# The first four attention chunks loaded on two queues, with three warming products instead of seven

## The chip, the cores and the metric

The kernel runs on one core of one Trainium2 chip. A core has TensorE (PE), VectorE (DVE), ScalarE (ACT), GpSimd (POOL) and SyncE (SP); each works through its own list of instructions in order. SyncE and ScalarE also issue DMAs, each on a hardware queue of its own. The metric is the device time of one execution in microseconds.

## The reference

Inputs q, k, v have the shape (4, 8, 576, 64): batch, heads, tokens, head size. The first stage is attention with a decay for each head and no softmax; two feed-forward layers follow, on 2304 tokens with 512 columns.

```python
scores = (1 / sqrt(64)) * q @ k^T
ret = scores * where(rel >= 0, gamma_h ** rel, 0)      # gamma_h = 1 - 2 ** (-5 - h)
x = (ret @ v).transpose(0, 2, 1, 3).reshape(2304, 512)
h = x @ moe_w_in                                       # 512 -> 2048
y = softplus(h) @ moe_w_out                            # 2048 -> 512
r = relu(y @ moe2_w_in)                                # 512 -> 2048
out = (r * r) @ moe2_w_out                             # 2048 -> 512
```

The weights come as float64 and are passed as pairs of 32-bit words; the kernel turns them into 32-bit parts itself. The launch also passes q and k stacked by dims (qk_t), k and v stacked by tokens (kv), and one small array of constants.

## The kernel before

Attention runs in chunks of 128 tokens, two pieces of 64 (s = 0, 1), over 8 heads. It is done in its recurrent form: each chunk has scores inside the chunk, a masked product with v, and a state that is carried to the next chunk. The first feed-forward layer takes its tokens in three tiles of 512, 384 and 384, and the remaining tokens go through a block later. The first tile needs chunks 0 to 3, so these are done ahead of everything else, in an order written out by hand (the block under `tc.manual_schedule()`, lines 1431 to 1510). Later chunks are loaded by `load_chunk` into a ring and worked in between the products of the feed-forward layer.

For an early chunk c:

- `early_qk(c)` (L1267) loads 512 KB of q and k in two DMAs: the lower four heads go to partitions 0 to 63, the upper four to partitions 64 to 127. `early_kv(c)` (L1276) loads 512 KB, k in column block 0 and v in block 1, in one DMA over 128 partitions. All of these are on SyncE's queue.
- `early_scores(c)` (L1281) makes 32 products on PE from both halves of qk. Even chunks write the tile pb, odd ones two other banks.
- `early_mask(c)` (L1304) multiplies the scores by the causal mask on VectorE; `early_v(c)` (L1297) scales v.
- `early_states(c)` (L1317) adds k^T v to the state on PE; ScalarE copies it (`kept`, L1329).
- `early_carried(c)` and `early_o(c)` make the output po on PE, from the kept state and from the masked scores. The tile po has one buffer, which `spread_rows` uses first, under the name rows.
- `early_x(c)` (L1352) multiplies po by a table in cst on VectorE (L1361), and ScalarE rounds the result (xh, L1366); `early_low(c)` makes the rest (xl, L1372).

The tables in cst are made on the chip. Two rows of constants are loaded (rows_in, L1442), `spread_rows` (L1407) spreads them over the partitions with eight products, ScalarE copies the result out (L1420, L1421), and `make_xw` on VectorE (L1248) and `scalar_xw` on ScalarE (L1426) make the tables of the later pieces.

`keep_warm(n)` (L1228) makes n products of a zero tile into a bank that nobody reads. There are six ahead of the scores of chunk 0 and one behind `spread_rows`.

Behind the chunks' loads SyncE issues the first three loads of w_in (L142, by `pump_load(3)`) and the loads of chunk 4 (L430). `begin_words` and what it starts turn a loaded piece of weights into words: two instructions on ScalarE (L172, L173), two on VectorE (L178, L181, tile ct), then a rounding on ScalarE (L226) and a difference on VectorE (L227). The first products of the feed-forward layer are in `early_g1` (L1391) and `g1` (L594).

Each DMA of the two hardware queues counts its landing on one of eight semaphores, which it takes in turn.

Of the kernel before, what the change touches and what calls it, by code (L numbers as in the profile page):

```python
# [18 lines left out]
CN = 64  # L19
# [30 lines left out]
C_ONE, C_UP, C_VW, C_MASK, C_XW = 0, 1, 2, 74, 138  # L50
# [4 lines left out]
def kernel(  # L55
# [26 lines left out]
    nc = tc.nc  # L82
# [261 lines left out]
    def pump_load(upto):  # L344
        while n_load[0] < min(upto, len(loads)):
            load_w(*loads[n_load[0]])
            n_load[0] += 1
# [72 lines left out]
    LO, HI = slice(0, P // 2), slice(P // 2, P)  # L420
# [5 lines left out]
    def load_chunk(c, queue=nc.sync):  # L426
        if c < NPR:
            new_chunk(c)
            for i, src in ((0, qk_t), (2, kv)):
                queue.dma_start(  # L430
                    out=chunk[c][:, i:i + 2],
                    in_=src[2 * c:2 * c + 2].rearrange("s p i h c -> (s p) i h c"),
                )
# [794 lines left out]
    def keep_warm(count, n=512):  # L1228

        for _ in range(count):  # L1230
            nc.tensor.matmul(
                cold[:, :n], lhsT=warm[:, :P], rhs=warm[:, :n], start=True, stop=True
            )
# [11 lines left out]
    def make_xw(m, n):  # L1245


        nc.vector.scalar_tensor_tensor(  # L1248
            out=later[:, m - 1:m - 1 + n],
            in0=cst[:, x_first].rearrange("p (a b) -> p a b", a=KD).unsqueeze(1)  # L1250
            .to_broadcast([P, n, KD, CN]),
            scalar=1.0,
            in1=times[:, m - 1:m - 1 + n].unsqueeze(3).to_broadcast([P, n, KD, CN]),
            op0=ALU.mult, op1=ALU.mult,
        )
# [4 lines left out]
    qks, kvs, mixed, kept_s, pbs, pos, xs_of = {}, {}, {}, {}, {}, {}, {}  # L1260
    causal = first_pool.tile([P, P], F32, tag="causal", name="causal", bufs=1)

    def early_tiles(c):
        qks[c] = first_pool.tile([P, 2, 2, HH, CN], F32, tag=f"qk{c}", name="qk", bufs=1)
        kvs[c] = first_pool.tile([P, 2, H, CN], F32, tag=f"kv{c}", name="kv", bufs=1)

    def early_qk(c):  # L1267
        for g, half in enumerate((LO, HI)):
            nc.sync.dma_start(
                out=qks[c][half].rearrange("p i s h c -> p i s (h c)"),  # L1270
                in_=qk_t[2 * c:2 * c + 2].rearrange("s p i h c -> p i s (h c)")[
                    ..., g * HH * CN:(g + 1) * HH * CN
                ],
            )

    def early_kv(c):  # L1276
        nc.sync.dma_start(
            out=kvs[c], in_=kv[2 * c:2 * c + 2].rearrange("s p i h c -> (s p) i h c")
        )

    def early_scores(c):  # L1281
        if c % 2:
            pb = pbs[c] = [ps_h.tile([P, 512], F32, tag=f"h{g}", name="pb") for g in range(2)]
        else:
            pb = ps_head.tile([P, 2, 512], F32, tag="pb", name="pb", bufs=1)
            pbs[c] = [pb]
            pb = [pb[:, g] for g in range(2)]
        for hh in range(HH):
            for s, to in enumerate((LO, HI)):
                for g, rows in enumerate((LO, HI)):  # L1290
                    nc.tensor.matmul(
                        pb[g][to, hh * P:(hh + 1) * P],
                        lhsT=qks[c][rows, 1, s, hh, :], rhs=qks[c][rows, 0, :, hh, :],
                        start=True, stop=True, skip_group_check=True,
                    )

    def early_v(c):  # L1297
        t = kvs[c][:, 1]
        w = vw[:, 2 * c * H:(2 * c + 1) * H]
        nc.vector.tensor_tensor(  # L1300
            out=t, in0=t, in1=w.unsqueeze(2).to_broadcast([P, H, D]), op=ALU.mult
        )

    def early_mask(c):  # L1304
        mixed[c] = first_pool.tile([P, H, P], F32, tag="mixed", name="mixed")
        for g, pb in enumerate(pbs[c]):
            n = H // len(pbs[c])
            if len(pbs[c]) == 1:
                pb = pb.rearrange("p g (h n) -> p (g h) n", n=P)
            else:  # L1310
                pb = pb.rearrange("p (h n) -> p h n", n=P)
            nc.vector.tensor_tensor(
                out=mixed[c][:, g * n:(g + 1) * n], in0=pb,
                in1=causal.unsqueeze(1).to_broadcast([P, n, P]), op=ALU.mult,
            )
# [29 lines left out]
    def early_o(c):  # L1345
        for hh in range(H):
            nc.tensor.matmul(
                early_po(c, hh), lhsT=kvs[c][:, 1, hh, :], rhs=mixed[c][:, hh, :],
                start=c == 0 and hh % HH < 2, stop=True, skip_group_check=True,
            )  # L1350
# [56 lines left out]
    def spread_rows():  # L1407
        rows = ps_head.tile([P, 2, 512], F32, tag="po", name="rows", bufs=1)
        to = [
            rows[:, 0, at:at + n * b].rearrange("p (a b) -> p a b", a=n)  # L1410
            for at, n, b in ((0, KD, CN), (256, SCN - 1, KD))
        ]
        for half in (LO, HI):
            one = slice(half.start, half.start + 1)
            for r, of in zip(to, (row[0][:, 0], row[0][:, 1:, :, 0])):
                nc.tensor.matmul(
                    r[half], lhsT=ones[one], rhs=of[one],
                    start=r is to[0], stop=True, skip_group_check=True,
                )
        nc.scalar.copy(cst[:, x_first].rearrange("p (a b) -> p a b", a=KD), to[0])  # L1420
        nc.scalar.mul(times, to[1], float(D) ** 0.5)  # L1421

    def scalar_xw(m, n):
        for m in range(m, m + n):
            for a in range(KD):
                nc.scalar.activation(  # L1426
                    out=later[:, m - 1, a], in_=cst[:, C_XW + a * CN:C_XW + (a + 1) * CN],
                    func=AF.Copy, scale=times[:, m - 1, a:a + 1],
                )

    with tc.manual_schedule():
        rows_in = xs.tile([P, SCN * KD * CN], F32, tag="xr", name="rows_in")
        for c in range(last):
            early_tiles(c)
        early_qk(0)
        for half in (LO, HI):
            nc.scalar.dma_start(out=cst[half, :C_XW], in_=consts[CN:P, :C_XW])
        early_kv(0)
        early_qk(1)
        early_kv(1)  # L1440
        for r in (0, CN):
            nc.scalar.dma_start(out=rows_in[r:r + 1], in_=consts[r:r + 1, C_XW:])  # L1442
        nc.scalar.preload_act_table_set("softplus")
        for c in range(2, last):
            early_qk(c)
            early_kv(c)
        pump_load(3)
        load_chunk(last)
        nc.vector.memset(causal[LO, CN:], 1.0)
        nc.vector.memset(causal[HI, :CN], 0.0)  # L1450

        for half, to, of, n in ((LO, 0, 0, SCN), (HI, 0, 1, SCN - 1), (HI, SCN - 1, 0, 1)):
            nc.vector.tensor_copy(
                vw[half, to * H:(to + n) * H], cst[half, C_VW + of * H:C_VW + (of + n) * H]
            )
        for s, half in enumerate((LO, HI)):
            nc.vector.tensor_copy(
                causal[half, s * CN:(s + 1) * CN], cst[half, C_MASK:C_MASK + CN]
            )
        keep_warm(6)  # L1460
        early_scores(0)
        row.append(rows_in.rearrange("p (m a b) -> p m a b", a=KD, b=CN))
        spread_rows()
        keep_warm(1)
        scalar_xw(4, 2)
        early_mask(0)
        early_v(0)
        make_xw(1, 1)
        early_scores(1)
        early_states(0)  # L1470
        early_mask(1)
        early_v(1)
        early_carried(0)
        early_o(0)
        early_x(0)
        early_scores(2)
        early_states(1)
        scalar_xw(6, 1)
        early_carried(1)
        early_o(1)  # L1480
        make_xw(2, 2)
        early_mask(2)
        early_v(2)
        early_x(1)
        scalar_xw(7, 2)
        early_scores(3)
        early_states(2)
        early_carried(2)
        early_o(2)
        early_low(0)  # L1490
        early_mask(3)
        early_v(3)
        begin_words()
        early_x(2)
        next(begun[0])
        early_low(1)
        early_states(3)
        early_carried(3)
        early_o(3)
        next(begun[0])  # L1500
        begun.clear()
        begin_words()
        early_g1(0)
        early_x(3)
        next_state(3, 1)
        begin_words()
        early_low(2)
        early_low(3)
        for made in begun:
            next(made)  # L1510
# [228 lines left out]
```

## Time and profile before

| what | value |
|---|---|
| runs | 817.22, 819.52, 819.86 us; median 819.52 |
| profiled execution | 820.17 us |
| its span, first to last instruction | 818.3 us |
| PE busy | 803.6 us, 98% of the span |
| DVE, ACT, POOL busy | 654.5, 402.5, 29.8 us |
| mean granted TensorE clock | 1.00 |
| DMA | 201.97 MB, mean 247 GB/s |

All times inside the span count from its first instruction. Busy times come from one profiled execution. An engine name with a q (SPq, ACTq) is that engine's sequencer, which issues DMAs; PEld is the loading of weights into PE, which overlaps with PE's products. A row of the timeline merges neighbouring instructions of one line and counts them (x2).

### The profile page before, as it was taken

How to read it: one execution, taken by the hardware profiler on the slowest of the kernel's cores; microseconds unless marked ns; L12 is line 12 of the kernel's file. 1: busy time of each engine (PE TensorE's matmuls, PEld its weight loads, DVE VectorE, ACT ScalarE, POOL GpSimd, SP SyncE). 2: the span in 40 equal slices, each digit the busy share in tenths (PEclk: the TensorE clock that was granted, in tenths of full speed). 3: DMA queues.
4: the chain of work that ended last, by engine and by line, in shares of the span. 5: the costliest groups of instructions: out<-in, count | busy, mean ns of one | idle time of the engine just before them, and what ended most of it. 6: DMA issues, size and time to landing. Idle time of an engine off the chain costs nothing.

```text
span 818.3 us, 16414 instructions
## 1 busy us (share of the span) xinstructions
PE 803.6 (98%) x5909; PEld 710.6 (87%) x5909; DVE 654.5 (80%) x1255; ACT 402.5 (49%) x781; POOL 29.8 (4%) x74
## 2 busy tenths in 40 slices
PE   8899999999899999999999999999999999999998
PEld 5678888988899888788888999988999988999887
DVE  4889886668547799977779698988798997897876
ACT  3888874555345456666666311554211554111553
POOL 0000111111110100000000000000000000000000
PEclk9999999999999999999999999999999999999999
DMA  9766776899557234459898987898988788987885
GB/s 238 267 195 210 258 248 229 291 306 322 204 195 238 94 116 146 140 171 348 280 318 298 314 278 252 268 291 281 296 253 249 250 274 264 298 248 249 254 271 172
DMA packets 124467, 201.97 MB, mean 247 GB/s; under 512 B 10850, under 2 KB 68834, under 8 KB 123618
## 3 DMA queue, kind: packets, MB, share of 16 engines
q1 hardware_dynamic: 118208, 179.87, 69.0%
q10 hardware_dynamic: 3620, 12.67, 4.7%
q0 software_dynamic: 2560, 8.39, 2.6%
q8 instruction: 47, 0.77, 0.4%
q14 instruction: 32, 0.26, 0.1%
HBM read 153.71 MB, written 47.19 MB: 245 GB/s over the span
## 4 chain that ended last, share of the span: by engine, by line
PE 74%; DMA 12%; DVE 8%; ACT 4%; issue 2%; SPq 0%; ACTq 0%; DVEq 0%
PE py L733 9%; PE py L806 9%; PE acc L628 8%; PE ph L594 8%; PE px L733 6%; PE pz L806 6%; PE px L806 6%; PE pz L733 6%; PE acc L1185 5%; PE py L1051 3%; DMA o2d<-ct 2%; DMA ring<-in_kv_dram 2%; DMA wo_raw<-in_moe_w_out_dram 2%; PE px L1051 2%; PE pz L1051 2%
## 5 line engine op out<-in xcount | busy, mean ns | idle before, releaser
L628 PE MATMUL acc<-gh,wo 128*128 128x384 f32 (+1 forms) x384 | 115.9, 362 | 0.6 <-ACT gh L612 0.6
L733 PE MATMUL py<-t,sring 128*128 128x384 f32 x432 | 88.3, 338 | 0.0
L594 PE MATMUL ph<-xh,wi 128*128 128x384 f32 (+1 forms) x376 | 80.4, 354 | 3.4 <-DVE ring L469 1.4
L628 PEld LDWEIGHTS acc<-gh,wo 128*128 128x128 f32 x384 | 70.8, 188 | 8.2 <-ACT gh L612 1.3
L733 PEld LDWEIGHTS py<-t,sring 128*128 128x128 f32 x432 | 74.8, 188 | 2.7 <-DVE uring L937 0.7
L594 PEld LDWEIGHTS ph<-xh,wi 128*128 128x128 f32 x376 | 67.0, 188 | 10.5 <-issue 2.0
L628 PE MATMUL acc<-gl,wo 128*128 128x384 f32 (+1 forms) x192 | 68.4, 356 | 1.3 <-DVE gl L613 1.3
L754 DVE TENSOR_TENSOR gl<-g,gh 128x384 fp32r<-128x384 f32 (+1 forms) x100 | 57.4, 575 | 11.2 <-ACT gh L786 8.0
L754 DVE TENSOR_TENSOR gring<-g,gring 128x384 fp32r<-128x384 f32 (+1 forms) x100 | 57.1, 575 | 11.5 <-ACT gring L786 9.0
L786 ACT CAST gh<-g 128x384 fp32r<-128x384 f32 x84 | 43.1, 515 | 46.6 <-PE px L806 16.7
L786 ACT CAST gring<-g 128x384 fp32r<-128x384 f32 x84 | 43.1, 514 | 40.3 <-PE py L806 16.4
L733 PE MATMUL pz<-t,sring 128*128 128x384 f32 x288 | 58.8, 334 | 0.0
L733 PE MATMUL px<-t,sring 128*128 128x384 f32 x288 | 58.3, 335 | 0.0
L933 ACT COPY uring<-px 128x384 f32<-128x384 f32 x24 | 11.5, 481 | 87.8 <-PE px L733 87.8
L754 DVE TENSOR_TENSOR g<-g 128x384 f32<-128x384 f32 x96 | 52.4, 554 | 1.4
L733 PEld LDWEIGHTS px<-t,sring 128*128 128x128 f32 x288 | 50.5, 188 | 0.6 <-ACT uring L933 0.5
L733 PEld LDWEIGHTS pz<-t,sring 128*128 128x128 f32 x288 | 50.8, 188 | 0.0
L469 DVE TENSOR_TENSOR ring<-pb,cst 64x256 f32<-64x256 f32 x56 | 23.6, 421 | 28.0 <-PE pb L459 16.4
L1185 PE MATMUL acc<-gring,wo 128*128 128x512 f32 x192 | 44.8, 389 | 0.0
L245 ACT CAST ct<-ct 128x512 fp32r<-128x512 f32 (+1 forms) x53 | 30.2, 570 | 28.1 <-DVE ct L181 15.6
L594 PE MATMUL ph<-xl,wi 128*128 128x384 f32 (+1 forms) x188 | 43.5, 352 | 0.0
L605 ACT ACTIVATE e<-ph 128x384 f32<-128x384 f32 (+1 forms) x48 | 25.2, 525 | 35.9 <-issue 19.5
(165 smaller groups left out, 1778.0 us busy)
## 6 DMA issues: line engine op xcount, KB each, us to landing
sring<-s2d SPq DMA_DIRECT2D x168, 256.0 KB, 3.3
sring<-o2d SPq DMA_DIRECT2D x168, 256.0 KB, 3.5
wi_raw<-in_moe_w_in_dram SPq DMA_DIRECT2D x32, 512.0 KB, 6.2
wo_raw<-in_moe_w_out_dram SPq DMA_DIRECT2D x32, 512.0 KB, 4.1
o2d<-ct SPq DMA_DIRECT2D x48, 256.0 KB, 3.2
s2d<-ct SPq DMA_DIRECT2D x33, 256.0 KB, 3.8
ring<-in_qk_t_dram ACTq DMA_DIRECT2D x12, 512.0 KB, 5.6
ring<-in_kv_dram ACTq DMA_DIRECT2D x12, 512.0 KB, 7.7
```

The costliest lines, as they stand in the source:

```text
L245: nc.scalar.copy(h, src)
L469: nc.vector.tensor_tensor(out=chunk[c][rows, 1, i * HH:(i + 1) * HH], in0=pb[of], in1=mask[of], op=ALU.mult)
L594: nc.tensor.matmul(ph[:, :n], lhsT=a, rhs=x, start=(j == 0), stop=(j == len(todo) - 1))
L605: nc.scalar.activation(out=g, in_=hps.pop(key)[:, :n], func=AF.Softplus)
L628: nc.tensor.matmul(acc[j][:, :n], lhsT=a, rhs=x, start=(begin and m == 0), stop=(end and m == 2))
L733: nc.tensor.matmul(ps, lhsT=a, rhs=x, start=(first and m == 0), stop=(m == len(todo) - 1), skip_group_check=True,)
L754: nc.vector.tensor_tensor(out=out, in0=a, in1=b, op=ALU.subtract)
L786: nc.scalar.copy(h, src)
L806: nc.tensor.matmul(blocks[m][:, :cols], lhsT=a[:, c], rhs=x, start=(first and p == n == 0), stop=(p == NP - 1 and n == len(todo) - 1), ski ...
L933: nc.scalar.copy(s1, px)
L1051: nc.tensor.matmul(ps, lhsT=a, rhs=x, start=(first and m == 0), stop=(m == len(todo) - 1), skip_group_check=True,)
L1185: nc.tensor.matmul(accs[half][j], lhsT=a[:, c], rhs=x, start=(begin and m == 0), stop=(end and m == 2),)
```

## The change

The lower heads of qk and all of k stay on SyncE's queue; the upper heads and v go to ScalarE's. kv becomes two DMAs of 256 KB. The two loads of rows_in are issued ahead of the kv of chunk 0 instead of behind the kv of chunk 1. `keep_warm(6)` becomes `keep_warm(3)`, and the `keep_warm(1)` behind `spread_rows` is gone. On ScalarE the order is then: upper qk of chunk 0, two loads of constants, two of rows, v of chunk 0, upper qk and v of chunk 1, the loading of the activation table (L1443), and upper qk and v of chunks 2 and 3; what ScalarE computes comes behind these.

```diff
     def early_qk(c):
-        for g, half in enumerate((LO, HI)):
-            nc.sync.dma_start(
+        for g, (half, queue) in enumerate(((LO, nc.sync), (HI, nc.scalar))):
+            queue.dma_start(
                 out=qks[c][half].rearrange("p i s h c -> p i s (h c)"),
                 in_=qk_t[2 * c:2 * c + 2].rearrange("s p i h c -> p i s (h c)")[
                     ..., g * HH * CN:(g + 1) * HH * CN
...
     def early_kv(c):
-        nc.sync.dma_start(
-            out=kvs[c], in_=kv[2 * c:2 * c + 2].rearrange("s p i h c -> (s p) i h c")
-        )
+        for i, queue in enumerate((nc.sync, nc.scalar)):
+            queue.dma_start(
+                out=kvs[c][:, i],
+                in_=kv[2 * c:2 * c + 2, :, i].rearrange("s p h c -> (s p) h c"),
+            )
...
         early_qk(0)
         for half in (LO, HI):
             nc.scalar.dma_start(out=cst[half, :C_XW], in_=consts[CN:P, :C_XW])
+        for r in (0, CN):
+            nc.scalar.dma_start(out=rows_in[r:r + 1], in_=consts[r:r + 1, C_XW:])
         early_kv(0)
         early_qk(1)
         early_kv(1)
-        for r in (0, CN):
-            nc.scalar.dma_start(out=rows_in[r:r + 1], in_=consts[r:r + 1, C_XW:])
         nc.scalar.preload_act_table_set("softplus")
...
-        keep_warm(6)
+        keep_warm(3)
         early_scores(0)
         row.append(rows_in.rearrange("p (m a b) -> p m a b", a=KD, b=CN))
         spread_rows()
-        keep_warm(1)
         scalar_xw(4, 2)
```

## Rows read from the trace of the kernel before

**Rows 1.** The page, engines: busy us (share of the span) and instructions.

```profile
PE 803.6 (98%) x5909; PEld 710.6 (87%) x5909; DVE 654.5 (80%) x1255; ACT 402.5 (49%) x781; POOL 29.8 (4%) x74
```

**Rows 2.** Windows: stretch, length, busy per engine (instructions), granted clock, DMA share, GB/s.

```profile
core 0: us, PE busy (x) PEld busy (x) DVE busy (x) ACT busy (x) POOL busy (x), PEclk, DMA share, GB/s
...
9.73:17.86 8.13, 7.73 (x168) 5.53 (x160) 6.42 (x9) 4.06 (x15) 0.00 (x0) 1.00 1.08 259
20.65:24.60 3.95, 3.62 (x89) 2.97 (x88) 3.16 (x5) 3.59 (x11) 0.00 (x0) 1.00 1.09 406
12.65:19.60 6.95, 6.47 (x143) 4.94 (x138) 5.68 (x9) 3.37 (x12) 0.00 (x0) 1.00 1.05 272
19.63:23.69 4.06, 3.71 (x94) 2.98 (x86) 2.81 (x5) 4.06 (x12) 0.00 (x0) 1.00 1.08 394
24.73:40.69 15.96, 13.70 (x79) 10.55 (x77) 13.72 (x21) 12.60 (x23) 0.00 (x0) 1.00 0.69 228
40.69:100.00 59.31, 59.31 (x489) 47.95 (x490) 53.30 (x88) 50.02 (x89) 1.57 (x4) 1.00 0.68 215
```

**Rows 3.** Chain of waits, first 80 us: start, us, what the end waited for.

```profile
2.29 7.44 DMA kv<-in_kv_dram
9.74 9.15 DMA qk<-in_qk_t_dram
...
40.69 2.83 PE ph L594 x11
```

**Rows 4.** Timeline, DMA issues of SyncE and ScalarE: start, us, engine, line.

```profile
0.74 1.20 ACTq L1437 DMA_DIRECT2D cst<-in_consts_dram  x2
0.74 1.50 SPq L1269 DMA_DIRECT2D qk<-in_qk_t_dram  x2
...
4.78 0.34 SPq L1277 DMA_DIRECT2D kv<-in_kv_dram  x1
```

**Rows 5.** DMA view, issues at 0.74, 1.52 and 4.78: KB, us to landing.

```profile
qk<-in_qk_t_dram SPq DMA_DIRECT2D x1, 256.0 KB, 4.0
...
qk<-in_qk_t_dram SPq DMA_DIRECT2D x1, 256.0 KB, 4.4
...
kv<-in_kv_dram SPq DMA_DIRECT2D x1, 512.0 KB, 9.0
```

**Rows 6.** Waits of SyncE's queue, 0 to 20 us: total, times, longest us.

```profile
SPq L1269 <- DMA kv<-in_kv_dram: 2.3, 1, 2.3
```

**Rows 7.** Timeline, PE and its weight loads, 1 to 10 us.

```profile
1.46 7.93 PE L1231 MATMUL cold<-warm 128*128 128x512 f32 x12 [1.46 <-DVE warm L1225]
...
5.88 0.34 PEld L1231 LDWEIGHTS cold<-warm 128*128 128x128 f32 x1 [0.52 <-issue]
...
6.65 0.19 PEld L1231 LDWEIGHTS cold<-warm 128*128 128x128 f32 x1 [0.43 <-issue]
...
9.31 1.10 PE L1291 MATMUL pb<-qk 64*64 64x128 f32 x32
```

**Rows 8.** Timeline, ScalarE and VectorE, 3 to 25 us.

```profile
3.04 1.28 ACT L1443 ACT_TABLE_LOAD   x1 [3.04 <-issue]
...
11.17 0.37 ACT L1420 COPY cst<-rows 128x256 f32<-128x256 f32 x1 [6.84 <-PE rows L1416]
11.44 0.20 ACT L1421 ACTIVATE times<-rows 128x32 f32<-128x32 f32 x1
...
12.23 0.42 DVE L1248 SCALAR_TENSOR_TENSOR cst<-cst,times 128x256 f32<-128x256 f32 x1
...
24.73 0.69 DVE L181 SCALAR_TENSOR_TENSOR ct<-wi_raw 128x512 uint32<-128x512 uint32 x1
```

## The prediction

> **What bounds the kernel now.** I read the page first. PE is busy 98% of the span [rows 1], so on the whole a microsecond is gained only where PE waits, or where work ahead of its stream ends sooner. The windows then cut the span: from 40.69 us on PE has no gap (59.31 busy of 59.31), while between 24.73 and 40.69 it is busy 13.70 of 15.96 and VectorE 13.72, ScalarE 12.60 [rows 2]. The chain of waits says what leads up to 40.69: a transfer of kv until 9.73, one of qk until 18.89, then work on VectorE and ScalarE until PE's first unbroken product at 40.69 [rows 3]. So the change is worth what it moves 40.69, and that shift should last: behind it the transfers are issued by what the engines finish and would move along.
>
> Two things hold the head of the kernel. One is the transfer rate. The loads of chunks 0 to 3 move 259 GB/s from 9.73 to 17.86, with the DMA share above 1; the weights behind them move 406 GB/s from 20.65 to 24.60 [rows 2]. kv of chunk 0 lands at 9.73 and kv of chunk 1 at 4.78 + 9.0 = 13.78, so a chunk of 1 MB takes 4.05 us [rows 3 to 5]; at the rate of the weights it is 1,048,576 / 406,000 = 2.58 us. The other is a limit on what is in flight: the load issued at 9.74 had waited 2.3 us for kv of chunk 0, which landed at 9.73 [rows 3, 6]. Counted over both queues in order of issue that load is the 14th and kv of chunk 0 the 6th; kv of chunk 1 is the 10th, and lands as the 18th is let go. So a load is issued only when the one eight places before it has landed, and the wait stands in the issuing engine's own stream.
>
> **The change part by part.**
>
> *Two queues.* Four chunks are 4 x 1.05 MB whichever queue they take. Between the two rates a chunk costs 2.58 to 4.05 us, so all of chunk 3 would be in at about 2 + 10.3 = 12.3 us if only the chunks moved, and no earlier than now at 259 GB/s. I take a rate near 400, because a lower half of the partitions then travels beside an upper half, and rows of weights over all partitions show that the engines can do it [rows 2]. But SyncE is done with its half early and goes on to the weights, which share the rate with ScalarE's half: 1 to 1.5 MB come between, another 2.6 to 3.9 us. Upper qk of chunk 3 then lands at 15 to 17 instead of about 19, still before PE can use it (below).
>
> The Trainium skill says why a half should be slow: "SBUF — State Buffer", section "Door 1: The DMA port swizzle", has partitions 0 to 63 reach only half of the ports. The 259 beside 406 GB/s agrees [rows 2]. But "DMA: Bandwidth & Descriptors", section "Rules for kernel authors", advises against two transfers to disjoint halves, as they would only take turns on the same engines; by it a chunk stays at 4.05 us and the sum is that of the third rival. No row of before shows two halves running side by side by design, so that is a rival below.
>
> *ScalarE's instructions.* It gains eight issues: upper qk and v of four chunks. An issue is 0.6 us where two take 1.20 to 1.50, down to 0.34 [rows 4]: 2.7 to 6 us. Now ScalarE does nothing from the end of the table load at 4.32 to L1420 at 11.17, where it waits 6.84 us for PE's rows [rows 8]; that idle time covers the issues themselves. It does not cover their waits: ScalarE works in order, and L1420 now stands behind its twelfth load, v of chunk 3. Behind L1420 are the tables that every x needs, and the buffer of the rows must be free before PE writes o(0).
>
> When is v(3) issued? If the two queues take places in turn, it waits for ScalarE's load four before it, v(1). The halves of qk(0) land at 4.74 and 5.9 now [rows 4, 5]; two rows later v(0) can be issued at about 5.5. A first 256 KB load takes 4.0 us from issue to landing [rows 5], the two behind it half of 406 GB/s each, 1.3 us: v(1) at 5.5 + 4.0 + 2.6 = 12.1, then the issue of v(3), and L1420 at about 12.6, 1.4 us later than now. The bounds: 10.3, if v(1) is not slowed by sharing and its predecessors are not held; and 15 or more, if v(3)'s place falls eight behind a weight (below). The table load, 1.28 us, is between v(1) and qk(2); it lies in the wait for v(1).
>
> *What goes behind L1420.* Now the distance from L1420 to the first weight's words, VectorE's ct at 24.73, is 13.56 us [rows 8]. With data present it is: L1420 and L1421 0.47 (11.17 to 11.64); the first table L1248 0.42, which no longer waits for the scaling of v(0), since that is done by then; VectorE's own work from 12.65 to 19.60, 5.68 busy of 6.95; ScalarE from 19.63 to 23.69, 4.06 without a gap [rows 2, 8]. That is 0.47 + 0.42 + 5.68 + 4.06 = 10.63, with handovers 10.7. So 2.86 us of waits and displaced work go, and ct comes sooner as long as L1420 starts before 11.17 + 2.86 = 14.0. What is late next is ScalarE's own order (casts, tables, words), so more cannot come at a fixed L1420.
>
> *Three warming products.* Seven cost nothing now: six are done at 9.39 and the scores of chunk 0 start at 9.31 [rows 7], and these are wanted no earlier while chunk 2 is on its way. With three, PE is free at about 1.46 + 3 x 0.85 = 4.0 and waits for qk(0) until about 5. What they buy is PE's level: its weight loads take 0.34 us up to 5.88 and 0.19 from 6.65 [rows 7], the lower and the higher of 1.2 and 2.4 GHz, though the granted clock reads 1.00 throughout [rows 2]; ahead of that rise PE had been busy 5.2 us without a gap. With three products it has gaps in this stretch. Bounds: 0, if the rise comes as now or before PE matters; at most 6.5, if the 6.47 us of PE between 12.65 and 19.60 [rows 2] all run at half speed. I take 0.5: PE is only second there, the scores run twice as long at the lower level and so fill the gaps, and the rise took 5 us now.
>
> *Rows and constants.* Both constant loads now stand behind upper qk(0), some 0.7 us later; the masks that need them are not due before scores(0) is done. k and v as separate loads have rows of 2 KB instead of 4; the rows of w_in, 128 columns of 8 bytes, are 1 KB and run at about 400 [rows 2], so nothing is charged.
>
> *Sum.* -2.86 + 1.4 + 0.5 = -1.0 us (rounded). The profiled execution took 820.17, 1.87 more than its span, and so 819.2; it stands 0.65 above the median 819.52 of the runs, so against these 818.5.
>
> **The rivals.**
>
> *ScalarE is held too long (slower).* The place: L1420, behind the issue of v(3). The table load sits in ScalarE's stream alone, so SyncE gets ahead in the turn of places, and v(3) can stand eight behind a weight instead of v(1). The first weight is issued at about 8.5 then and, sharing, needs the 4.0 and another 1.3 to 2.6 us: 15 to 16. From 14.0 on it decides, each microsecond is lost: at 15.5, +1.5 and PE's 0.5 make 821.5. For: the wait at 9.74 shows that the limit binds now, on a queue with one kind of load [rows 6]. Against: SyncE, too, is held by the same places.
>
> *The full gain.* Queues free of each other, L1420 at 10.3, PE at its higher level in time: -2.86 - 0.9 = -3.8, 815.8. For: 6.84 us of idle time on ScalarE [rows 8]. Against: v(1) has to land by 10, and 9.73 is when kv(0) does now.
>
> *The halves take turns after all.* 4.2 MB of chunks and 1 MB of weights at 259 GB/s end at 2 + 20 = 22 us; upper qk(3) is in at about 22, some 3 us later than now, when it already is on the chain [rows 3]: +3, 822.5. This is also the case in which the change does not do what it says. Against: weights at 406 GB/s on the same engines.
>
> *PE stays low through o(1).* 5.2 us of continuous work before the rise, as now [rows 7], at half speed is 2.6 more than the forecast's 0.5 has: 818.5 + 2.1 = 820.6.
>
> **How the numbers follow.** Forecast 0.50, between no gain and 2.4 us (817.1 to 819.5); held too long 0.14; full gain 0.20; taking turns 0.07; PE low 0.09. About 0.3%, 2.5 us, is what a measurement here tells from no change: below 817.06 faster, above 821.98 slower. Faster: the full gain and a little of the forecast's end, 0.25. Slower: nearly all of the turns, half of the long hold, a little of PE low, 0.15. Within 0.60. The range takes in the full gain nearly and the holds: 816.0 to 822.0.
>
> **What would show it.** Right: the loads of the first 15 us at well over 300 GB/s, with ScalarE's queue carrying 2.1 MB more; ScalarE's issues with waits up to about 12; L1420 at 12 to 13 and no longer released by PE's rows; VectorE without waits from the masks on; ct near 23.7 instead of 24.73, and PE's unbroken stream from about 39.7. Wrong: L1420 past 14, or before 11; weight loads of 0.34 us on PE after 13; chunk transfers still near 259 GB/s; or a head that moves while the rest of the span does not keep the shift.

## The result and the profile after

| | before | after |
|---|---|---|
| median of the runs beside each other | 817.48 us (6 runs) | 824.89 us (6 runs, 823.73 to 826.83) |
| ratio | | 1.0086, 95% interval 1.0066 to 1.0107 |
| profiled execution, span | 820.17, 818.3 us | 824.92, 823.1 us |
| mean granted TensorE clock | 1.00 | 0.991 |

The change costs 0.9%, where 818.5 us was forecast, 1.0 us less than before. Of e7's six runs below one took 988.67 us at a granted clock of 0.75 and is left out of its row. The page's busy times hardly moved (compare [rows 1]), so the time is not more work but a later start of the same work:

```profile
PE 801.9 (97%) x5901; PEld 712.0 (86%) x5901; DVE 655.0 (80%) x1255; ACT 403.5 (49%) x781; POOL 29.4 (4%) x74
```

The code behind the change has moved by up to two lines: L1420 of before is L1422 of after, L1416 is L1418, L1291 is L1293, L1277 is L1278. Timeline of after, VectorE and PE, as in [rows 8] and [rows 3]:

```profile
30.53 0.69 DVE L181 SCALAR_TENSOR_TENSOR ct<-wi_raw 128x512 uint32<-128x512 uint32 x1
```

```profile
1.45 5.16 PE L1231 MATMUL cold<-warm 128*128 128x512 f32 x6 [1.45 <-DVE warm L1225]
6.54 1.10 PE L1293 MATMUL pb<-qk 64*64 64x128 f32 x32
8.70 1.63 PE L1418 MATMUL rows<-rows_in,ones 1*64 1x256 f32 x8 [1.05 <-DMA rows_in<-in_consts_dram]
10.25 0.68 PE L1293 MATMUL pb<-qk 64*64 64x128 f32 x2
16.67 1.98 PE L1293 MATMUL pb<-qk 64*64 64x128 f32 x30 [5.74 <-DMA qk<-in_qk_t_dram]
...
46.52 1.88 PE L594 MATMUL ph<-xh,wi 128*128 128x512 f32 x7 [0.35 <-DVE wi L227]
```

The first weight's words, ct, start 5.80 us later than before (24.73), and PE's unbroken stream 5.83 us later (40.69). From there to the end of the execution both take about the same, 824.92 - 46.52 = 778.4 and 820.17 - 40.69 = 779.5 us. So the head is where to look. Two things stand out. The scores of chunk 1 (two products at 10.25, thirty at 16.67) wait 5.74 us for the upper half of qk. And ScalarE's first copy comes at 19.47 instead of 11.17 (timeline, ScalarE's issues and its first work):

```profile
0.74 0.74 ACTq L1269 DMA_DIRECT2D qk<-in_qk_t_dram  x1
1.51 1.53 ACTq L1439 DMA_DIRECT2D cst<-in_consts_dram  x2
3.07 1.53 ACTq L1441 DMA_DIRECT2D rows_in<-in_consts_dram  x2
8.58 0.37 ACTq L1278 DMA_DIRECT2D kv<-in_kv_dram  x1
8.99 0.64 ACTq L1269 DMA_DIRECT2D qk<-in_qk_t_dram  x1
...
15.50 0.34 ACTq L1278 DMA_DIRECT2D kv<-in_kv_dram  x1
16.65 0.60 ACTq L1269 DMA_DIRECT2D qk<-in_qk_t_dram  x1
19.10 0.33 ACTq L1278 DMA_DIRECT2D kv<-in_kv_dram  x1
19.47 0.37 ACT L1422 COPY cst<-rows 128x256 f32<-128x256 f32 x1 [7.70 <-DMA qk<-in_qk_t_dram]
```

The bracket of the last row names a landing of qk, but the row above it says what L1422 stood behind: the issue of v(3) at 19.10. Meanwhile SyncE (its timeline) had all of its half out by 8.0 and went on to the weights:

```profile
5.47 0.60 SPq L1269 DMA_DIRECT2D qk<-in_qk_t_dram  x1
6.41 0.33 SPq L1278 DMA_DIRECT2D kv<-in_kv_dram  x1
6.79 0.60 SPq L1269 DMA_DIRECT2D qk<-in_qk_t_dram  x1
7.67 0.37 SPq L1278 DMA_DIRECT2D kv<-in_kv_dram  x1
8.09 3.54 SPq L142 DMA_DIRECT2D wi_raw<-in_moe_w_in_dram  x3
```

The DMA view gives what each issue took to land (KB, us): the weights issued at 8.09 and 10.15, and upper qk(1), issued at 8.99:

```profile
wi_raw<-in_moe_w_in_dram SPq DMA_DIRECT2D x1, 512.0 KB, 7.4
...
wi_raw<-in_moe_w_in_dram SPq DMA_DIRECT2D x1, 512.0 KB, 8.9
...
qk<-in_qk_t_dram ACTq DMA_DIRECT2D x1, 256.0 KB, 7.6
```

8.09 + 7.4 = 15.5 is when v(2) is issued, and 10.15 + 8.9 = 19.05 is when v(3) is. A load's place is its number in the order in which the loads take the eight semaphores, counted over both queues. By place the first weight is the 14th load and v(2) the 22nd, the second weight the 17th and v(3) the 25th: eight places each time. v(0) is the 15th and stands eight behind a load of rows_in, which PE's row at 8.70 shows landing only then.

Last the rate. From 4 to 12 us the windows of after read 291, 286, 259 and 252 GB/s, 272 on average and hardly more than the 259 of one queue [rows 2]. But the DMA view from 2 to 12 us (packets, MB, share of the 16 DMA engines; q1 is SyncE's queue, q10 ScalarE's) shows that one queue did most of it:

```profile
q1 hardware_dynamic: 1801, 2.24, 90.0%
q10 hardware_dynamic: 436, 0.35, 13.4%
```

Two halves were seldom under way together here, so this stretch does not tell whether they add up; e3, below, does. The granted clock is in the windows of after (columns as in [rows 2]):

```profile
8.00:10.00 2.00, 1.30 (x7) 0.88 (x8) 1.57 (x3) 0.00 (x0) 0.00 (x0) 0.89 1.08 259
10.00:12.00 2.00, 0.94 (x5) 0.47 (x3) 0.00 (x0) 1.28 (x1) 0.00 (x0) 0.50 1.06 252
12.00:14.00 2.00, 0.00 (x0) 0.00 (x0) 0.00 (x0) 0.00 (x0) 0.00 (x0) 0.50 1.08 392
...
20.00:24.00 4.00, 3.78 (x88) 3.15 (x90) 4.00 (x7) 3.42 (x13) 0.00 (x0) 1.00 1.06 354
```

### The profile page after: what moved, and what is told of

Read it like the earlier page. It is cut to its first block, busy times and chain, and to the rows that moved or that the text cites. A ratio compares the mean times of both kernels' runs of the same rounds, so it can differ in the third digit from the quotient of the medians.

```text
span 823.1 us, 16403 instructions
## 1 busy us (share of the span) xinstructions
PE 801.9 (97%) x5901; PEld 712.0 (86%) x5901; DVE 655.0 (80%) x1255; ACT 403.5 (49%) x781; POOL 29.4 (4%) x74
## 4 chain that ended last, share of the span: by engine, by line
PE 50%; DMA 3%; DVE 1%; ACT 1%; issue 0%; SPq 0%; DVEq 0%; ACTq 0%
PE py L733 9%; PE py L806 9%; PE px L733 6%; PE pz L806 6%; PE pz L733 6%; PE px L806 6%; PE acc L1185 6%; DMA wo_raw<-in_moe_w_out_dram 2%; PE py L1051 1%; DMA wo<-wod 1%; PE px L1051 1%; PE pz L1051 0%; DVE ct L181 0%; DMA o2d<-ct 0%; DVE ct L252 0%
## 5 line engine op out<-in xcount | busy, mean ns | idle before, releaser
L754 DVE TENSOR_TENSOR gl<-g,gh 128x384 fp32r<-128x384 f32 (+1 forms) x100 | 57.5, 576 | 10.9 <-ACT gh L786 7.7
L933 ACT COPY uring<-px 128x384 f32<-128x384 f32 x24 | 11.6, 481 | 87.6 <-PE px L733 87.6
L1185 PE MATMUL acc<-gh,wo 128*128 128x512 f32 x128 | 42.0, 400 | 1.9 <-DMA wo<-wod 1.9
```

The source lines that it names most:

```text
L754: nc.vector.tensor_tensor(out=out, in0=a, in1=b, op=ALU.subtract)
L933: nc.scalar.copy(s1, px)
L1185: nc.tensor.matmul(accs[half][j], lhsT=a[:, c], rhs=x, start=(begin and m == 0), stop=(end and m == 2),)
```

## The experiments

Each ran in five rounds beside the kernel before. "Words" is the start of the first ct, "stream" that of PE's unbroken stream, both in us of the profiled execution.

| run | median us | ratio to before, 95% interval | first copy | words | stream |
|---|---|---|---|---|---|
| before (profile above) | | | 11.17 | 24.73 | 40.69 |
| after | 824.89 | 1.0086 [1.0066, 1.0107] | 19.47 | 30.53 | 46.52 |
| after again (e7) | 826.12 | 1.0103 [1.0072, 1.0135] | 20.88 | 32.52 | 48.47 |
| after, seven warming (e1) | 823.44 | 1.0049 [1.0030, 1.0067] | 20.42 | 32.20 | 48.18 |
| the same again (e8) | 825.08 | 1.0073 [1.0048, 1.0098] | 22.36 | 33.95 | 49.93 |
| before, three warming (e2) | 818.26 | 0.9996 [0.9977, 1.0016] | 8.92 | 24.40 | 40.37 |
| after, constants on GpSimd (e3) | 817.06 | 0.9976 [0.9957, 0.9995] | 14.01 | 24.53 | 40.50 |
| after, two chunks split (e4) | 823.61 | 1.0046 [1.0031, 1.0061] | 11.73 | 28.95 | 44.93 |
| after, upper half on GpSimd (e5) | 824.60 | 1.0070 [1.0042, 1.0098] | 9.31 | 33.11 | 49.07 |
| before, full width (e6) | 816.85 | 0.9979 [0.9963, 0.9995] | 10.32 | 22.11 | 38.09 |
| after, full width (g3) | 822.70 | 1.0053 [1.0034, 1.0073] | 18.73 | 29.62 | 45.76 |
| before, one full load (f1) | 814.74 | 0.9961 [0.9947, 0.9976] | 11.43 | 23.23 | 39.21 |
| f1, three warming (f2) | 813.31 | 0.9942 [0.9923, 0.9962] | 8.41 | 19.26 | 35.24 |
| g3, constants on GpSimd (h1) | 813.81 | 0.9947 [0.9929, 0.9966] | 9.73 | 22.68 | 38.66 |

**The two parts of the change apart (e1, e2).** e1 is the kernel after with the warming products of before, e2 the kernel before with those of after.

```diff
-        keep_warm(3)
+        keep_warm(6)
...
         spread_rows()
+        keep_warm(1)
```

> The changed kernel with the seven warming products put back (six and one); the loads stay on two queues. Theory 1 (ScalarE's loads and its first copy are held by the turn of the eight places): stays 5 to 7 us above before, the first copy of the rows on ScalarE still at 19 to 20 us, the scores of chunk 1 still waiting for qk until 16 to 17. Theory 2 (the lost time is TensorE at its lower level for want of warming): back to within 1.5 us of before. Theory 3 (half loads and rows of 2 KB move slower): as theory 1 in time, but with the chunk loads at or below 259 GB/s.

> The kernel before with three warming products instead of seven; its loads unchanged. Theory 1: within 1.5 us of before, since the data of chunks 2 and 3 still come at 14.8 and 18.9 us. Theory 2: 3 to 6 us slower, with TensorE's weight loads at 0.34 us after 13 us. Theory 3: no change.

With seven products the two queues are still slower than before; with three, one queue is as before within 0.2%. So the loss belongs to the loads. The split of kv and the move of rows_in ahead of v(0) were not tried by themselves. In e2 the granted clock does fall to 0.50 (its window), and the words come no later for it (24.40 against 24.73):

```profile
12.00:14.00 2.00, 2.00 (x38) 1.67 (x32) 1.07 (x2) 0.01 (x1) 0.00 (x0) 0.50 1.10 284
```

**Places (e3).** The four small loads leave ScalarE's queue for GpSimd's, which uses semaphores of its own; the chunk loads then alternate between SyncE and ScalarE in the order of places.

```diff
-            nc.scalar.dma_start(out=cst[half, :C_XW], in_=consts[CN:P, :C_XW])
+            nc.gpsimd.dma_start(out=cst[half, :C_XW], in_=consts[CN:P, :C_XW])
...
-            nc.scalar.dma_start(out=rows_in[r:r + 1], in_=consts[r:r + 1, C_XW:])
+            nc.gpsimd.dma_start(out=rows_in[r:r + 1], in_=consts[r:r + 1, C_XW:])
```

> The changed kernel with the two loads of constants and the two of rows issued by GpSimd, which takes its places from a pool of its own; so ScalarE's v and upper qk of chunk 1 are among the first eight and v of chunk 3 waits for a load of chunk 2, not for a weight. Theory 1: v of chunk 0 lands before 9 us, ScalarE's first copy starts at 11 to 13, and the time is 2 us below to 1 us above before (815.5 to 818.5). Theory 2: still 3 to 6 us slower than before. Theory 3: chunk loads at 259 GB/s or less and qk of chunk 3 at 20 us or later, 1 to 3 us slower.

The loss is gone; the kernel is even 0.24% faster than before. PE's scores of chunk 1 start at 10.10 now, and the two landmarks of the prediction (timelines of ScalarE and VectorE) read:

```profile
14.01 0.37 ACT L1422 COPY cst<-rows 128x256 f32<-128x256 f32 x1 [8.82 <-DMA qk<-in_qk_t_dram]
```

```profile
24.53 0.69 DVE L181 SCALAR_TENSOR_TENSOR ct<-wi_raw 128x512 uint32<-128x512 uint32 x1
```

Two queues and the split of kv are still there, so neither is the loss by itself. This run also tests the rate, since both queues now carry chunk loads from the start. Its windows, and the DMA view of the two halves of qk(0), both issued at 0.74:

```profile
4.00:6.00 2.00, 2.00 (x4) 0.67 (x2) 0.00 (x0) 1.19 (x1) 0.00 (x0) 1.00 1.09 277
6.00:8.00 2.00, 1.96 (x34) 0.86 (x32) 0.44 (x3) 0.00 (x0) 0.00 (x0) 1.00 1.09 324
8.00:10.00 2.00, 1.30 (x8) 0.86 (x8) 1.86 (x5) 0.00 (x0) 0.00 (x0) 1.00 1.07 343
10.00:12.00 2.00, 2.00 (x35) 1.66 (x33) 0.37 (x1) 0.00 (x0) 0.00 (x0) 0.55 1.13 244
12.00:14.00 2.00, 1.18 (x20) 0.93 (x16) 0.00 (x0) 0.00 (x0) 0.00 (x0) 0.60 1.08 249
14.00:16.00 2.00, 1.46 (x32) 1.29 (x36) 1.48 (x3) 1.95 (x9) 0.00 (x0) 1.00 1.09 240
```

```profile
qk<-in_qk_t_dram ACTq DMA_DIRECT2D x1, 256.0 KB, 5.2
qk<-in_qk_t_dram SPq DMA_DIRECT2D x1, 256.0 KB, 4.1
```

From 4 to 16 us that is 280 GB/s on average, where the same windows of before average 256: a small gain, and an uneven one. Side by side the halves landed at 4.8 and 5.9, no sooner than at 4.74 and 5.9 one behind the other on one queue [rows 4, 5].

**ScalarE held, or data late (e4, e5).** Both let ScalarE go. e4 leaves only chunks 0 and 1 split; e5 gives the upper halves and v to GpSimd's queue (`nc.gpsimd` for `nc.scalar` in both places, for all four chunks).

```diff
-        for g, (half, queue) in enumerate(((LO, nc.sync), (HI, nc.scalar))):
+        for g, (half, queue) in enumerate(((LO, nc.sync), (HI, (nc.scalar, nc.sync)[c >= 2]))):
...
-        for i, queue in enumerate((nc.sync, nc.scalar)):
+        for i, queue in enumerate((nc.sync, (nc.scalar, nc.sync)[c >= 2])):
```

> The changed kernel with chunks 2 and 3 wholly on SyncE's queue; only chunks 0 and 1 are loaded on two. ScalarE's stream is free behind v of chunk 1 and the table load, but v of chunk 0 and upper qk of chunk 1 keep their late places. Theory 1: ScalarE's first copy starts at 10 to 12 us instead of 19.5, the scores of chunk 1 wait until 13 to 16, and the time is 1 to 4 us above before, less than half of the change's loss. Theory 2: still 5 to 7 us above before. Theory 3: about as theory 1.

> The changed kernel with the upper heads and v on GpSimd's queue instead of ScalarE's; ScalarE issues the constants and rows alone, and GpSimd's loads take places of their own. Theory 1 (place and hold): ScalarE's first copy at 8.5 to 11 us, the scores of chunk 1 not later than 11, and the loss of the change is gone: 815.5 to 819 beside 818. Theory 3 (halves side by side are no faster than one after the other): chunk loads still at 240 to 290 GB/s, qk of chunk 3 at 17 to 20 us. If the halves do add up, 350 GB/s or more and qk of chunk 3 by 15.

In e4 ScalarE's first copy is at 11.73, close to before, yet the words are 4.22 us later than before, because PE (its timeline) still waits for upper qk(1), to the same 16.5:

```profile
16.52 1.98 PE L1293 MATMUL pb<-qk 64*64 64x128 f32 x30 [4.99 <-DMA qk<-in_qk_t_dram]
```

So late data alone make some 4.2 of the 5.8 us; the hold of ScalarE is worth the other 1.6 at most in this reading. The two are not strictly additive, as e4 also orders the later loads differently, and by the medians, taken on different chips, e4 keeps about half of the loss (0.46 of 0.86%). Theory 1 expected the loss to be gone in e5, and it was not. ScalarE is free at 9.31, but GpSimd's issues (its timeline) come late, and PE's scores of chunk 1 wait to 14.33 and those of chunk 2 to 22.65:

```profile
1.28 0.80 POOL L1269 DMA_DIRECT2D qk<-in_qk_t_dram  x1 [0.84 <-POOLq L1716]
2.03 0.62 POOL L1278 DMA_DIRECT2D kv<-in_kv_dram  x1
6.40 0.68 POOL L1269 DMA_DIRECT2D qk<-in_qk_t_dram  x1 [3.74 <-issue]
7.75 0.56 POOL L1278 DMA_DIRECT2D kv<-in_kv_dram  x1 [0.67 <-issue]
14.59 0.69 POOL L1269 DMA_DIRECT2D qk<-in_qk_t_dram  x1 [6.28 <-issue]
```

So e5 repeats the wait for late data by another cause, and says nothing of the eight places.

**The same again (e7, e8).** e7 is the kernel after once more, e8 is e1 once more, on one chip.

> The changed kernel once more, on the chip of the next one. Theory 1: 0.6 to 0.95% above before. Only as the reference for the next.

> The changed kernel with seven warming products, once more, beside the changed kernel on one chip. Theory 1: within 0.2% of it. Theory 2: 0.3 to 0.4% below it, as the two runs on different chips (1.0049 and 1.0086) would have it.

e7 confirms the loss. In both pairs the kernel with seven products is the quicker one by about 0.3%, but the intervals overlap, and the profiles have its words later, not sooner: what the warming products do in the kernel after stays open.

**Width (e6, g3).** The launch lays q and k of chunks 0 to 3 out so that the q of a chunk is one load over all 128 partitions, and k another. e6 has both on SyncE, as before; g3 has q on SyncE and k on ScalarE, in the kernel after.

```diff
-        for g, half in enumerate((LO, HI)):
+        for i in range(2):
             nc.sync.dma_start(
-                out=qks[c][half].rearrange("p i s h c -> p i s (h c)"),
...
+                out=qks[c][:, i].rearrange("p s h c -> p (s h c)"),
+                in_=qk_t[2 * c:2 * c + 2, :, i].rearrange("s p h c -> (s p) (h c)"),
```

> The kernel before with qk of the early chunks laid out by the launch so that each of its two loads of 256 KB covers all 128 partitions (q, then k, rows of 2 KB) instead of a lower and an upper half; all on SyncE's queue, the same bytes, the same number of loads, seven warming products. Theory 3: a chunk takes 2.6 to 2.9 us instead of 4.05, the chunk loads run at 370 to 406 GB/s, qk of chunk 3 lands at 13.5 to 15; time 1 to 3 us below before, for ScalarE's first copy is still held to 11.2 by TensorE's seven products. If the half width is not the cause: 259 GB/s and no change in time.

> The changed kernel with its two queues and three warming products, but a chunk of q and k is laid out by the launch so that a load covers all 128 partitions: q on SyncE's queue, k on ScalarE's, 256 KB each. Separates the rate of half-width loads from the order of places. Theory 1 (the order of places, most of the loss): loads run near 400 GB/s, yet k of chunk 1 still stands behind SyncE's whole half, so scores of chunk 1 still wait and ScalarE's first copy is past 14; at 2.6 us a MB the lag behind 1.5 MB more shrinks from 5.8 to some 3: about 820 to 822. Theory 2 (half-width rate, most of the loss): first copy at 12 to 14, the first weight's words at 22 to 25, 815 to 818.

Same bytes, same queue, and e6's windows read

```profile
8.00:10.00 2.00, 2.00 (x39) 1.23 (x39) 0.36 (x1) 0.00 (x0) 0.00 (x0) 1.00 1.04 411
10.00:12.00 2.00, 2.00 (x36) 1.18 (x36) 1.80 (x3) 1.64 (x7) 0.00 (x0) 1.00 1.03 409
```

where the same windows of before read 258 and 257. The rows of q and k are also longer in e6, 2 KB instead of 1; but the weights have rows of 1 KB and ran at about 400 GB/s [rows 2]. So it is the half width that keeps the loads of before at 259. In g3 the loads reach that rate from 4 to 6 us (375) and from 12 us on, but from 6 to 12, when SyncE's queue carries 1.43 of 1.67 MB, its windows read 243, 287 and 303 GB/s; why is not shown. ScalarE and PE are nearly as late as in the kernel after (its timelines):

```profile
8.00:10.00 2.00, 0.41 (x2) 0.32 (x3) 0.40 (x1) 0.00 (x0) 0.00 (x0) 1.00 0.98 287
...
16.00:18.00 2.00, 2.00 (x36) 1.67 (x38) 0.00 (x0) 0.00 (x0) 0.00 (x0) 0.50 1.08 411
```

```profile
15.88 1.98 PE L1291 MATMUL pb<-qk 64*64 64x128 f32 x32 [5.54 <-DMA qk<-in_qk_t_dram]
...
18.73 0.37 ACT L1420 COPY cst<-rows 128x256 f32<-128x256 f32 x1 [6.21 <-DMA qk<-in_qk_t_dram]
```

The time keeps 0.5 of the 0.9%, and beside e6, which has the same loads of q and k on one queue, g3 is 0.7% slower (1.0053 / 0.9979). That is nearer to theory 1: most of the loss is not the rate but the places.

**What beats both (f1, f2, h1).** f1 is e6 with q and k of a chunk in one load of 512 KB, f2 is f1 with three warming products, h1 is g3 with e3's edit.

```diff
+        nc.sync.dma_start(
+            out=qks[c].rearrange("p i s h c -> p (i s h c)"),
+            in_=qk_t[2 * c:2 * c + 2].rearrange("s p i h c -> (s p) (i h c)"),
+        )
...
-        keep_warm(6)
+        keep_warm(3)
...
-        keep_warm(1)
```

> The kernel before with q and k of an early chunk as one load of 512 KB over all 128 partitions (laid out so by the launch), all on SyncE, seven warming products. Beside the run with two 256 KB loads (816.85) it halves the issues and takes fewer places. If the rate alone counts: the first weight's words at about 22, the time 816 to 817. If places or issues count as well: another 0.5 to 1.5 us sooner.

> The same with three warming products, none behind the scores of chunk 0. Theory A (once the data come early, warming products are what PE's first scores wait for): ScalarE's first copy at 7 to 9 instead of about 10, the words 1 to 3 us sooner than with seven, 813 to 815.5. Theory B (PE's lower clock takes it back): the granted clock shows 0.5 in part of the first 15 us, the words no sooner, 816 to 818.

> The changed kernel (two queues, three warming products) with both faults mended at once: q and k laid out by the launch for loads over all 128 partitions, and the four loads of constants and rows issued by GpSimd instead of ScalarE, so that the two queues start their chunk loads together. If the order of places and the half-width rate are all there is to the loss, ScalarE's first copy comes at about 9 to 11, the first weight's words at 19 to 22, and the time is that of one queue with full-width loads (813 to 816): two queues then neither cost nor gain. If splitting over two queues gains by itself once both are mended: below 812. If it still costs by itself (waits in ScalarE's stream, clock at 0.5): 817 or more.

All three beat before; f2 and h1 by 0.5 to 0.6%, with intervals that overlap. So with both faults mended two queues neither cost nor gain as far as the medians tell, though in the profiles h1's words come 3.4 us later than f2's. In f1 the scores of chunk 0 stand behind the warming products (PE's timelines of f1 and f2):

```profile
9.57 1.10 PE L1288 MATMUL pb<-qk 64*64 64x128 f32 x32
```

```profile
5.80 1.10 PE L1288 MATMUL pb<-qk 64*64 64x128 f32 x32
```

Three products let them start 3.8 us sooner, without a lower clock (1.00 in all of f2's first 40 us), and the words come 4.0 us sooner in the profiled executions. The medians show only 1.4 us, within their intervals. f2's profiled execution was its fastest, 809.91, in a spread of 6.8 us (f1: 2.4); why f2 varies more is open, as only one of its executions has a trace. In h1 q and k run side by side at the full rate, 404, 396, 406, 402 and 376 GB/s in the windows from 4 to 14 us, and those of chunk 0, issued at 0.74, land at 4.2 and 4.4 (DMA view). ScalarE is let go in time. One of the windows, and ScalarE's timeline:

```profile
8.00:10.00 2.00, 1.91 (x28) 1.38 (x32) 1.89 (x3) 0.27 (x2) 0.00 (x0) 1.00 1.05 406
```

```profile
9.32 0.36 ACTq L1276 DMA_DIRECT2D kv<-in_kv_dram  x1
9.73 0.37 ACT L1420 COPY cst<-rows 128x256 f32<-128x256 f32 x1 [5.82 <-PE rows L1416]
```

## Why the prediction was wrong

The forecast was -2.86 + 1.4 + 0.5 = -1.0 us for the words. By the same terms the trace has: ScalarE's first copy at 19.47 instead of 11.17, **+8.30** where 1.4 stood; and from there to the words 11.06 us instead of 13.56, -2.50 where -2.86 + 0.5 = -2.36 stood. Together +5.80. So the sum failed in one term. That the other came out so near is in part luck: with L1420 as early as 11.73 (e4) the words still came at 28.95, for want of data that the prediction took as present.

**The failed step: when v(3) is issued, and with it L1420.** The prediction said "If the two queues take places in turn, it waits for ScalarE's load four before it, v(1)", had v(0) issued at 5.5 and L1420 at 12.6. The places don't alternate. ScalarE has five loads ahead of v(0), and SyncE has its half and a weight placed before it: v(0) is the 15th of all, issued at 8.58; v(2) and v(3) wait for weights. The same order shows in e7 (v(0) issued at 8.50, first copy at 20.88). With the places interleaved (e3) the loss is gone. The argument set against the hold, that SyncE is held by the same places, overlooked what stands eight ahead of SyncE's fifth to eighth loads, upper qk(0), k(0) and the two loads of constants, all landed by 7.65: SyncE's half was out while ScalarE stood behind rows_in.

**A wait that the prediction did not have.** It asked when qk of chunk 3 is in, not of chunk 1. Upper qk(1) was issued at 8.99, landed at 16.6, and PE stood for 5.74 us. By e4's words this is the larger part of the loss, by its median about half.

**The rate.** "I take a rate near 400, because a lower half of the partitions then travels beside an upper half" was wrong: in e3, with halves on both queues, it is 280 GB/s from 4 to 16 us, and the halves of qk(0) landed no sooner. Here the Trainium skill was right against my reading of [rows 2]: "DMA: Bandwidth & Descriptors", section "Rules for kernel authors", holds that two transfers to disjoint partition halves take turns, and that one transfer over 128 partitions should be used instead; e6's 411 and 409 GB/s agree with that too. But the third rival priced this at +3 us and that was not so: e3 is little above the low rate and faster than before, g3 has the high rate for most of its head and is slower.

**A misread row.** "1.46 + 3 x 0.85 = 4.0" took a warming product for one instruction. [rows 7] counts twelve for six products, and in after PE was busy with three (x6) until 6.6. Upper qk(0) landed at 5.5, so the scores of chunk 0 came about 1 us late, ahead of longer waits.

**The rivals.** "ScalarE is held too long" had the mechanism, with 0.14 for it. It put v(3) eight behind the first weight, landing at 15 to 16; that weight landed at 15.5, but it held v(2), and v(3) stood behind the second, at 19.1. It also counted only the copy and not chunk 1's scores. "The full gain" was refuted by the same rows. "PE stays low" came true as a state, the granted clock being 0.50 from 10 to 18 us, but e1 has seven products, much of the loss, and a clock of 0.50 as well (14 to 20 us); what the lower clock adds in the kernel after was not taken apart.

**What held.** The path behind L1420, 10.7 us with data present: 10.5 in e3, 10.9 in g3 and in f2, 11.1 in after; it was longer in e7 (11.6) and h1 (13.0). The break-even of 14.0: e3's copy at 14.01 gives words at 24.53, 0.20 sooner than before. The eight places. The shift of the head lasts to the end, to about 1 us between before and after. Over all the profiles, though, the time less the start of the stream lies between 774.7 (f2) and 779.5 us (before), so a shift of a few us need not show in full. The 0.5 us for the warming products is below what e2 resolves (-1.9 to +1.3 us).

## What to carry to other kernels

Splitting loads over two queues that draw on one limited set of places moves work from one order to another: write down the order of places, and for each load what stands eight ahead of it, small constants and later weights included; a load issued from a computing engine holds that engine's work for as long. Loads on disjoint halves of the partitions gained little side by side (280 against 256 GB/s); lay the data out so that one load covers all partitions. And look at the first consumer, chunk 1, not only at the last load.

## What was not expected of the hardware

- GpSimd's 256 KB loads came in pairs (e5): each issue from 6.40 on came about 0.3 us after the landing of the load two before it (landings at 6.08, 7.44, 14.28, 15.12; issues at 6.40, 7.75, 14.59, 15.42). Its four loads of at most 34.5 KB in e3 and h1 went out one behind the other. What limits it isn't shown.
- PE's granted clock, 1.00 until 8 us in after, was 0.89 from 8 to 10 us, with PE busy 1.30 of 2.00, and 0.50 (the lower level, 1.2 GHz) from 10 to 18, where PE stood idle from 12 to 16. It stayed there for some time in work: thirty score products took 1.98 us at 16.67 in after, where thirty-two took 1.10 at 6.54. It was back at 1.00 (2.4 GHz) from 20 us. In e2 and e3 shorter dips cost nothing that shows in the words.
